# Float64 weights as a clipped 16-bit top and a 32-bit rest, and new lists of steps, in a sparse-attention and gated-MLP kernel

## The chip, the cores and the metric

The kernel runs on one core of a Trainium2 chip. The metric is the device time of one execution in microseconds (us). Engines are named PE (matrix), DVE (vector), ACT (scalar), POOL (GpSimd) and SP, which here only issues transfers.

## What is computed

```python
# attention: batch 8, 8 heads, 576 tokens, 64 wide
mask_local   = (rel >= 0) & (rel < 32)                      # heads 0 to 3
mask_strided = (rel >= 0) & (pos_k % 32 == pos_q % 32)      # heads 4 to 7
attn = softmax(where(mask, q @ k.T / 8, -1e9));  x = attn @ v      # x: 8 x 576 x 512
# gated MLP on x
h = gelu_tanh(x @ w_in)                    # 512 -> 1024
u, v = h[..., :512], h[..., 512:]
v_n = layernorm(v) * g_ln
v_s = einsum('ts,bsd->btd', w_sg, v_n) + b_sg
out = x + (u * v_s) @ w_out                # 512 -> 512
```

`w_in` and `w_out` arrive as float64. No engine reads float64 here: the kernel sees each weight as two 32-bit words and makes a float32 from them, then a rounded high part and a low part (`wih`/`wil`, `woh`/`wol`) for three-product matmuls.

## The kernel before

The eight batches run one behind the other, and the attention of the next batch is woven into the MLP of this one. Every step has a short name. Three lists of names, written out by hand in the file, fix the order: `START` (attention of batch 0, conversion of the weights, MLP of batch 0, attention of batch 1), `CYCLE` (MLP of batch b, attention of b+1; batches 1 to 6) and `LAST` (MLP of batch 7). Each engine works off its own instructions in the order of the list; transfers follow the list's order across the queues of SP and ACT. A `^` at a name picks the other choice of engine, queue or PSUM pool (`loads()`, `slow()`, `psum()`); `=`, `-`, `+` only say which batch is meant.

Names that matter below:

- `cl`, then `ca` to `ch`, convert one of 16 pieces of weight: 0 to 7 are 128x512 values of `w_in` (0 to 3 feed the `v` matmuls, 4 to 7 the `u` matmuls), 8 to 15 are 128x256 values of `w_out`. The piece's raw words lie in tile `stage` (0 to 7) or `cs` (8 to 15), the result in `cv`, `cx` or `cxl`. `cl` loads, `cg` writes the high part on ACT, `ch` the low part on POOL (or DVE with `^`).
- `TP`/`TC` turn rows of q and k on PE and copy them out (`qT`, `kT`); `SS`, `SL` are strided and local scores (`ss`, `sa`, `sr`); `MK`, `MX`, `SB`, `EX`, `SU`, `ML` are the softmax on `sms` and `sml`; `PL`, `PS` transpose the weights of attention (`ptl`, `pts`); `VA`/`VX`/`VY`, `PV`/`PW` multiply by v (`ol`, `os`); `XH`, `XL` write high and low parts of x (`xt`).
- In the MLP: `v1`, `v2`, `v` the v matmuls, `g` their gelu (`hv`), `ls`, `lr`, `lm`, `lh`, `ll` the layer norm (`lr` is a chain of 14 tiny POOL instructions that gives `y`; `lh` on ACT and `ll` on DVE write tile `vg`, and tile `t` for the last 64 tokens), `u` the u matmuls, `ug` their gelu on ACT, `s` the token-mixing matmuls (`sg`), which read `vg` and last of all `t`, `o` the output matmuls. A matmul's PSUM tile has two buffers in each of two pools, so the third use of a pool waits until the first was read.
- `LV`, `LQ`, `LP` load v, q and k.

The old conversion in numbers per piece: DVE takes the exponent field (`ca`), ACT rebiases it (`cb`), DVE puts the sign in and masks the mantissa (`cc`, two instructions), ACT scales it to 1.m (`cd`), the low word is added (`ce`, one DVE instruction, or ACT and POOL with `^`), and a product joins mantissa and exponent (`cf`, POOL or DVE).

Of the kernel before, what the change touches and what calls it, by code (L numbers as in the profile page):

```python
# [30 lines left out]
TC-:5 we=^ cd=:6 SS-^:2 cl=^:7 wt=:1 EX-:5 ML-:4 TC^:2 SU-^:5 MK-:2 cg=:0 TZ:0 ch=:0 ce=^:6
ML-^:5 TP:3 ca=:4 TZ:1 MX-:2 ML-:3 wh=:1 TC:3 LV-:0 ca=:7 PL-:4 wm=:1 CL-^:4 cb=:4 PL-^:5 CL-:5
SB-^:2 LP:0 CM-:5 ch=:3 VX-:0 VY-:0 EX-:2 XR-:0 LV-:1 SU-:2 ML-^:2 cb=:7 TP^:0 XHa-:0 XLa-:0
TC:0 cb=:9 ce=^:8 cf=:8 TP:1 TC:1 PS-^:2 XHb-:0 cc=:9 XLb-:0 cf=^:6 cc=:4 CS-:2 cl=:5 SL^:0
ca=:5 SL:1 XD-:0 MK:0 VA-:1 XH-:1 XL-:1 cd=:4 cc=:7 LV-:2 PV-^:2 PW-:2 LP:2 cd=:9 XH-:2 ce=:9
wo= cb=:5 XR-:1 MX:0 PS-:3 SB:0 wp= CS-:3 XL-:2 XD-:1 va:0 XR-:2 vb:0 cd=:7 cl=^:13 TP^:4 TC:4
vc:0 LV-:3 PV-:3 cc=:5 EX:0 PW-:3 XH-^:3 ce=:4 cf=^:4 va:1 XL-:3 xt cg=:4 vd:0 g:0 XD-^:2 XR-:3
vb:1 ce=:7 LP:3 wl=^:0 cf=^:9 ls:0 TP:6 ch=:4 vc:1 cd=:5 ce=:5 LZ:1 cf=:7 cg=^:9 vd:1 ch=^:9
TP:7 lr^:0 v^:2 ca=^:13 TC:6 cg=:6 cf=^:5 g:1 TC:7 ls:1 cg=:7 cg=:5 cl=^:15 TP^:5 ch=:6 ch=^:5
SS^:3 ch=:7 TC:5 cb=:13 cc=^:13 u:2 vh XD-:3 vl TZ+:0 g:2 cd=:13 MK:3 lg= LV:1 ce=:13 lm:0  # L40
wt=^:0 cf=^:13 wl=^:4 rt cl=:10 lh:0 ls:2 lm:1 wh=:0 wm=:0 lr:1 lm:2 lh:1 SS:2 ug:2 u^:1 wl=:2
lr:2 ug:1 ll:0 ca=:10 wt=^:4 cb=:10 ca=:15 cb=:15 u:0 SU:0 wh=:4 cc=:10 cg=:8 wl=:3 cd=:10 wt=:2
LQ+:0 wm=:4 ug:0 ce=:10 cf=:10 MK:2 wh=:2 cc=^:15 wm=:2 cl=^:11 wt=^:3 wh=:3 lh:2 cg=:13 wm=:3
ML:0 ll:2 u:3 ll:1 cd=:15 ca=:11 PL:0 cb=:11 cc=:11 ch=:13 CL:0 ug:3 MX:3 s:3 sm:3 ce=^:15
cd=:11 ce=:11 s^:2 cf=:11 cg=:11 CM:0 cf=^:15 MX:2 SB^:3 SB^:2 s^:0 cg=:10 ch=^:11 sm:2 cl=^:12
ca=:12 s:1 EX:3 TZ+:1 sh:2 sl:2 SU:3 sh:3 cb=:12 LZ:0 LQ+:3 ch=:8 cc=:12 ch=^:10 sm:0 cl=:14
cg=:15 cd=:12 ca=:14 ce=^:12 cf=:12 sh:0 cg=:12 TQ+:0 LV:0 ML^:3 VA^:1 sm:1 sh:1 sl:1 XR:1 r
cb=:14 sl:3 cc=:14 EX:2 sl^:0 ch=^:15 LQ+:1 VA:0 PS:3 CS:3 o:0 ch=:12 cd=:14 o^:1 ce=:14 cf=^:14
# [53 lines left out]
def tile_sparse_attention_moe(  # L102
# [166 lines left out]
    def cv(i):  # L269
        pairs = conv[i].rearrange("p (n w) -> p n w", w=2)  # L270
        n = pairs.shape[1]
# [12 lines left out]
        return pairs[:, :, 0], pairs[:, :, 1], conv[i, "ex"]  # L284

    def cv_load(i):
        if i < 8:
            conv[i] = stage[:, i % 5]
        else:
            conv[i] = p1.tile([P, F2], I32, tag="ob", name=f"cs_{i}", bufs=2)  # L290
        loads().dma_start(conv[i], halves[i][0])

    def cv_field(i):

        w0, w1, ex = cv(i)
        dve.tensor_scalar(
            ex, w1, 20, 0x7FF, op0=ALU.logical_shift_right, op1=ALU.bitwise_and
        )

    def cv_exp(i):  # L300

        w0, w1, ex = cv(i)
        act.activation(ex, ex, AF.Relu, bias=ebias, scale=float(1 << 23))

    def cv_sign(i):

        w0, w1, ex = cv(i)
# [5 lines left out]
    def cv_one(i):  # L313

        w0, w1, ex = cv(i)
        act.activation(w1.bitcast(F32), w1, AF.Copy, bias=1.0, scale=float(2.0 ** -20))

    def cv_word(i):

        w0, w1, ex = cv(i)  # L320
        mf, low = w1.bitcast(F32), w0.bitcast(U32)
        if alt[0]:
            act.activation(w0.bitcast(F32), low, AF.Copy, scale=float(2.0 ** -52))
# [722 lines left out]
```

## Time and profile before

| | us |
|---|---|
| three runs | 574.88, 579.43, 582.8 (median 579.43) |
| the profiled execution | 579.7 |
| its span on the core | 577.5 |
| PE busy | 542.7 (94%) |
| DVE busy | 415.3 (72%) |
| ACT busy | 216.0 (37%) |
| POOL busy | 180.6 (31%) |

The span is what the trace covers; the 2.2 us around it are taken as fixed. All rows below have line L83, since one helper issues every instruction: they are told apart by the names of tiles.

### The profile page before, as it was taken

What the parts mean: (1) busy time and instruction counts of PE and PEld (TensorE: products, weight loads), DVE (VectorE), ACT (ScalarE), POOL (GpSimd) and SP (SyncE); (2) the same over time, 40 slices, a digit from 0 to 9 for tenths busy, and PEclk for the clock granted to TensorE, in tenths of its full rate; (3) what the DMA queues carried; (4) which work ended last, traced back from release to release, by engine and by line L of the source; (5) the groups of instructions that cost most, each with busy time, mean ns of one, the idle gap of its engine ahead of it and who ended that gap; (6) DMA issues with size and microseconds to landing.
All of it is one profiled execution on the core that took longest, in us unless ns stands there. A gap on an engine that the chain in (4) does not pass through costs nothing. (4 is left out here: it accounts for less than half of the span.)

```text
span 577.5 us, 17028 instructions
## 1 busy us (share of the span) xinstructions
PE 542.7 (94%) x7217; PEld 483.9 (84%) x7217; DVE 415.3 (72%) x702; ACT 216.0 (37%) x352; POOL 180.6 (31%) x431
## 2 busy tenths in 40 slices
...
GB/s 244 237 203 118 140 154 82 181 151 154 181 34 53 161 173 143 42 114 155 165 75 49 165 173 139 42 135 137 168 79 51 159 188 37 0 139 143 1 0 92
DMA packets 253678, 70.09 MB, mean 121 GB/s; under 512 B 237793, under 2 KB 239329, under 8 KB 253602
## 3 DMA queue, kind: packets, MB, share of 16 engines
...
q10 hardware_dynamic: 82032, 21.31, 16.5%
...
## 5 line engine op out<-in xcount | busy, mean ns | idle before, releaser
L83 PE MATMUL sg<-wsh,vg 128*128 128x288 f32 x512 | 112.8, 296 | 0.7 <-DVE wst L83 0.5
L83 PE MATMUL u<-xt,wih 128*128 128x288 f32 x512 | 105.5, 301 | 7.1 <-ACT u L83 6.9
L83 PE MATMUL o<-woh,vg 128*128 128x512 f32 x288 | 95.2, 400 | 0.0
L83 PEld LDWEIGHTS u<-xt,wih 128*128 128x128 f32 x512 | 83.1, 190 | 9.8 <-ACT u L83 8.4
L83 PEld LDWEIGHTS sg<-wsh,vg 128*128 128x128 f32 x512 | 85.7, 188 | 1.4 <-issue 0.7
L83 PE MATMUL v<-wih,xt 128*128 128x512 f32 x256 | 84.5, 400 | 0.1
L83 PE MATMUL u<-xt,wil 128*128 128x288 f32 x256 | 76.3, 298 | 1.0 <-DVE wil L83 1.0
L83 PE MATMUL sg<-wsl,vg 128*128 128x288 f32 x256 | 75.4, 295 | 0.0
L83 PEld LDWEIGHTS o<-woh,vg 128*128 128x128 f32 x288 | 53.6, 188 | 13.4 <-DVE vg L83 2.6
L83 PEld LDWEIGHTS v<-wih,xt 128*128 128x128 f32 x256 | 48.6, 190 | 10.8
L83 PE MATMUL o<-wol,vg 128*128 128x512 f32 x144 | 56.3, 391 | 0.0
L83 PE MATMUL v<-wil,xt 128*128 128x512 f32 x128 | 50.3, 393 | 0.0
L83 PEld LDWEIGHTS u<-xt,wil 128*128 128x128 f32 x256 | 48.7, 190 | 1.2 <-DVE wil L83 1.2
L83 DVE TENSOR_TENSOR ob<-o,xn 128x512 f32<-128x512 f32 x32 | 22.0, 688 | 37.7 <-PE o L83 34.1
L83 PEld LDWEIGHTS sg<-wsl,vg 128*128 128x128 f32 x256 | 48.3, 189 | 0.0
L83 ACT CAST vg<-gt 128x576 fp32r<-128x576 f32 (+2 forms) x48 | 22.2, 511 | 57.7 <-DVE gt L83 57.7
L83 DVE TENSOR_TENSOR gt<-sg,u 128x576 f32<-128x576 f32 x32 | 23.8, 743 | 23.3 <-PE sg L83 20.7
L83 DVE BATCH_NORM_STATS2 bnst<-hv 128x6 f32<-128x512 f32 (+1 forms) x40 | 27.0, 675 | 18.1 <-ACT hv L83 18.1
...
L83 POOL MEMSET v<- 32x128 f32 x16 | 3.1, 198 | 97.9 <-PE os L83 70.6
L83 ACT ACTIVATE vg<-hv,y 128x512 fp32r<-128x512 f32 x32 | 20.7, 712 | 33.6 <-POOL y L83 31.6
L83 DVE TENSOR_TENSOR vg<-gt,vg 128x576 fp32r<-128x576 f32 (+2 forms) x45 | 23.2, 554 | 12.1 <-ACT vg L83 12.1
...
## 6 DMA issues: line engine op xcount, KB each, us to landing
...
```

The lines of the kernel that those rows point to most:

```text
L83: ins = self.tc.keep_in_program_order(op(*args, **kwargs))
```

## The change

The transfer of a raw piece now lands two bytes further on, so that of each float64 the top 16 bits lie in one int16 and the middle 32 bits in one aligned word. The tiles `stage` and `cs` are two words longer per partition for that. The top is clipped (`ck`: POOL, or DVE with `^`), a second instruction subtracts the clipped from the bounded top and so rebiases exponent and sign at once (`cc`, DVE), ACT scales the difference by 2^19 into an int32 (`ca`), ACT scales the middle word by 2^-13 into an int32 (`cd`), and POOL adds the two int32 (`ce`). `cg` and `ch` stay.

```diff
-    stage = p1.tile([P, 5, 2 * F2], I32, tag="vg", name="stage")
+    stage = p1.tile([P, 5, 2 * F2 + 2], I32, tag="vg", name="stage")
...
-        loads().dma_start(conv[i], halves[i][0])
+        n = halves[i][0].shape[1]
+        loads().dma_start(conv[i].bitcast(I16)[:, 1 : 2 * n + 1], halves[i][0].bitcast(I16))
+
+    def cv_clip(i):
+        mid, top, ex = cv(i)
+        slow().tensor_scalar(
+            ex.bitcast(F32), top, -14336.0, 14336.0, op0=ALU.max, op1=ALU.min
+        )
+
+    def cv_signed(i):
+        mid, top, ex = cv(i)
+        dve.scalar_tensor_tensor(
+            ex.bitcast(F32), top, -18432.0, ex.bitcast(F32), op0=ALU.max, op1=ALU.subtract
+        )
...
-        dve.tensor_scalar(
-            ex, w1, 20, 0x7FF, op0=ALU.logical_shift_right, op1=ALU.bitwise_and
-        )
...
-        act.activation(ex, ex, AF.Relu, bias=ebias, scale=float(1 << 23))
...
-        dve.scalar_tensor_tensor(
-            ex, w1, -(1 << 31), ex, op0=ALU.bitwise_and, op1=ALU.bitwise_or
-        )
-        dve.tensor_scalar(w1, w1, 0xFFFFF, None, op0=ALU.bitwise_and)
...
-        act.activation(w1.bitcast(F32), w1, AF.Copy, bias=1.0, scale=float(2.0 ** -20))
...
-        if alt[0]:
-            act.activation(w0.bitcast(F32), low, AF.Copy, scale=float(2.0 ** -52))
-            pool.tensor_tensor(mf, mf, w0.bitcast(F32), op=ALU.add)
-        else:
-            dve.scalar_tensor_tensor(mf, low, float(2.0 ** -52), mf, op0=ALU.mult, op1=ALU.add)
...
-        slow().tensor_tensor(val, w1.bitcast(F32), val, op=ALU.mult)
...
+        act.activation(ex, ex.bitcast(F32), AF.Copy, scale=float(1 << 19))
...
+        act.activation(mid, mid.bitcast(U32), AF.Copy, scale=float(2.0 ** -13))
...
+        pool.tensor_tensor(ex, ex, mid, op=ALU.add)
```

All three lists are written anew. Of `CYCLE`, the first two lines:

```diff
-v1:0 r SL:0 SL:1 TQ:3 v1:1 MK:0 xt MX:0 v2:1 SB^:0 g:1 ls^:1 v2:0 g:0 v^:2 vh lr:1 ls:0 u:2 ug:2
-u^:3 vl^ lm:0 g:2 TQ:2 lr:0 LQ+:0 lh:0 lm^:1 SS^:2 lh:1 SS^:3 ug:3 u^:0 ug:0 ls^:2 MK^:3 ll:1
+v1:0 r SL:0 TQ:3 SL:1 MK:0 xt v1:1 MX:0 v2:1 SB^:0 g:1 ls^:1 lr:1 v2:0 v^:2 g:0 vh ls:0 u:2 vl^
+ug:2 lr:0 lm:0 g:2 TQ:2 LQ+:0 SS^:3 u^:3 lm^:1 ug:3 SS^:2 lh:0 lh:1 u^:0 ug:0 ls^:2 MK^:3 lr:2
```

What that does to the engines is shown at three places. A row is the instruction, its output tile, its inputs and its shape; the last number of a tile's name only counts tiles.

First place, ACT at the end of `START`, where batch 1's MLP begins. Before, the five transfers of `v_0` (the last two are shown) stand ahead of the table load and the gelu `hv_1`:

```order
L83 DMA v_0_1903<-in_v_dram 64x8x64
L83 DMA v_0_1903<-in_v_dram 32x2x64
L83 ACT_TABLE_LOAD
L83 ACTIVATE hv_1_2067<-v_1_2032 128x1024
L83 ACTIVATE hv_0_2088<-v_0_1939 128x1024
```

Now, at the same place on ACT:

```order
L83 DMA out_dram<-ob_1_1866 128x512
L83 DMA out_dram<-ob_0_1878 128x512
L83 ACT_TABLE_LOAD
L83 ACTIVATE hv_1_2030<-v_1_2002 128x1024
L83 ACTIVATE hv_0_2077<-v_0_1902 128x1024
```

The five `v_0` transfers have moved to SP's queue, between those of `v_2` and `rawq_2`; it is the only batch for which they stood on ACT.

Second place, ACT in `CYCLE` (batch 1; batches 2 to 6 read alike), from the gelu of `u_2` to that of `u_1`, before:

```order
L83 ACTIVATE u_2_2150<-u_2_2125 128x576
L83 ACTIVATE hv_2_2099<-hv_2_2099 64x512
L83 ACTIVATE vg<-hv_0_2088,y_0_2186 128x4x128 x2
L83 ACTIVATE vg<-hv_1_2067,y_1_2102 128x4x128 x2
L83 ACTIVATE u_3_2284<-u_3_2152 128x576
L83 ACTIVATE u_0_2311<-u_0_2286 128x576
L83 ACTIVATE t_97<-hv_2_2099,y_2_2322 64x512
L83 ACTIVATE t_94<-hv_2_2099,y_2_2322 64x512
L83 ACTIVATE u_1_2376<-u_1_2340 128x576
```

And now:

```order
L83 ACTIVATE u_2_2114<-u_2_2088 128x576
L83 ACTIVATE hv_2_2079<-hv_2_2079 64x512
L83 ACTIVATE u_3_2210<-u_3_2183 128x576
L83 ACTIVATE vg<-hv_0_2077,y_0_2117 128x4x128 x2
L83 ACTIVATE vg<-hv_1_2030,y_1_2040 128x4x128 x2
L83 ACTIVATE u_0_2274<-u_0_2249 128x576
L83 ACTIVATE u_1_2330<-u_1_2303 128x576
L83 ACTIVATE t_97<-hv_2_2079,y_2_2283 64x512
L83 ACTIVATE t_94<-hv_2_2079,y_2_2283 64x512
```

The gelu of `u_3` has moved ahead of the four `vg` writes, and that of `u_1` ahead of the two `t` writes. On DVE the low part of `t` now stands ahead of the mask of `ss_2` instead of behind it, and on PE `ss_3` ahead of `u_3`.

Third place, DVE in `START`, from behind the product that `ptl` waits for (`sml` by `sr_5`) to the product that `pts` waits for (`sms_98` by `sr_2`), before:

```order
L83 TENSOR_SCALAR cv_522<-stage 128x512
L83 TENSOR_REDUCE mx_2_526<-sms_98 100x16
L83 TENSOR_SCALAR cv_538<-stage 128x512
L83 TENSOR_TENSOR wsl<-wsgT_492,wsh 128x4x128
L83 TENSOR_TENSOR wst<-wsgT_492,wsh 64x128
L83 TENSOR_TENSOR sms_98<-sms_98,mx_2_526 100x16x36
L83 COPY ptl_5_557<-ptl_8_555 128x128
L83 STREAM_TRANSPOSE xs_0_606<-ol_0_568 128x576
L83 TENSOR_REDUCE sr_2_613<-sms_98 100x16
L83 TENSOR_SCALAR sr_2_613<-sr_2_613 100x16
L83 RECIPROCAL sr_2_613<-sr_2_613 100x16
L83 TENSOR_TENSOR sms_98<-sms_98,sr_2_613 100x16x36
```

And now:

```order
L83 TENSOR_TENSOR sml_330<-sml_330,sr_5_494 128x640
L83 TENSOR_SCALAR cv_513<-stage 128x512
L83 TENSOR_TENSOR sms_98<-sms_98,mx_2_500 100x16x36
L83 SCALAR_TENSOR_TENSOR cv_513<-stage,cv_513 128x512
L83 TENSOR_SCALAR cv_527<-stage 128x512
L83 SCALAR_TENSOR_TENSOR cv_527<-stage,cv_527 128x512
L83 TENSOR_TENSOR wsl<-wsgT_446,wsh 128x4x128
L83 TENSOR_TENSOR wst<-wsgT_446,wsh 64x128
L83 TENSOR_REDUCE sr_2_590<-sms_98 100x16
L83 TENSOR_SCALAR sr_2_590<-sr_2_590 100x16
L83 RECIPROCAL sr_2_590<-sr_2_590 100x16
L83 TENSOR_TENSOR sms_98<-sms_98,sr_2_590 100x16x36
```

The maximum `mx_2` has moved ahead of the first product; the copy and the transpose have moved behind the second, and two conversions' second steps have come in between.

In all, DVE has 36 conversion rows where it had 74, ACT 48 where it had 53, POOL 28 where it had 22.

## Rows read from the trace of the kernel before

**Rows 1.** The page, part 1: busy us, share of the span, instructions.
```profile
PE 542.7 (94%) x7217; PEld 483.9 (84%) x7217; DVE 415.3 (72%) x702; ACT 216.0 (37%) x352; POOL 180.6 (31%) x431
```
**Rows 2.** Windows: stretch, length, busy us per engine, PE clock, DMA share, GB/s.
```profile
10.00:50.00 40.00, 28.93 (x593) 24.19 (x594) 37.76 (x68) 24.19 (x45) 18.19 (x22) 1.00 0.96 214
157.60:161.00 3.40, 3.40 (x17) 3.40 (x17) 3.32 (x5) 1.33 (x2) 1.28 (x4) 0.55 0.50 78
```
**Rows 3.** What PE waited for, 0 to 100 us: total us, times, longest.
```profile
PE ptl L83 <- DVE sml L83: 1.9, 1, 1.9
...
PE pts L83 <- DVE sms L83: 1.3, 1, 1.3
...
PE u L83 <- DVE wil L83: 1.0, 1, 1.0
PE turnk L83 <- DVE sml L83: 0.9, 1, 0.9
PE ptl L83 <- POOL sml L83: 0.8, 1, 0.8
...
PE sg L83 <- DVE wst L83: 0.5, 1, 0.5
```
**Rows 4.** What PE waited for, 100 us to the end.
```profile
PE u L83 <- ACT u L83: 6.9, 5, 3.4
```
**Rows 5.** Timeline of batch 1's MLP: start, us, engine, instruction, idle before.
```profile
133.79 4.35 ACTq L83 DMA_DIRECT2D v<-in_v_dram  x5
...
139.47 1.94 ACT L83 ACTIVATE hv<-v 128x1024 f32<-128x1024 f32 x2
...
153.24 2.56 ACT L83 ACTIVATE vg<-hv,y 128x512 fp32r<-128x512 f32 x4 [7.10 <-POOL y L83]
...
160.26 0.74 DVE L83 SCALAR_TENSOR_TENSOR t<-hv,y,t 64x512 fp32r<-64x512 f32 x1
...
136.81 0.62 PE L83 MATMUL v<-wih,xt 128*128 128x512 f32 x2
...
156.38 0.54 PE L83 MATMUL u<-xt,wih 128*128 128x288 f32 x2 [3.40 <-ACT u L83]
...
162.78 0.29 PE L83 MATMUL sg<-wsh,t 128*128 128x288 f32 x1
```
**Rows 6.** Timeline of batch 3's MLP, the same places, as a later batch runs.
```profile
291.38 0.63 ACT L83 ACTIVATE u<-u 128x576 f32<-128x576 f32 x1
...
291.38 0.74 DVE L83 SCALAR_TENSOR_TENSOR t<-hv,y,t 64x512 fp32r<-64x512 f32 x1
...
287.49 0.53 PE L83 MATMUL u<-xt,wih 128*128 128x288 f32 x2 [0.69 <-ACT u L83]
...
292.36 0.29 PE L83 MATMUL sg<-wsh,t 128*128 128x288 f32 x1
```
**Rows 7.** Groups of DVE instructions by form, 0 to 165 us: count, busy us, mean ns.
```profile
L83 DVE TENSOR_TENSOR cv<-stage,cv 128x512 f32<-128x512 f32 x6 | 6.0, 1008 | 0.1
L83 DVE TENSOR_SCALAR cv<-stage 128x512 int32<-128x512 int32 x8 | 5.6, 702 | 1.4 <-DMA stage<-in_moe_w_in_dram 1.4
L83 DVE SCALAR_TENSOR_TENSOR stage<-stage 128x512 f32<-128x512 uint32 x6 | 4.0, 675 | 0.0
...
L83 DVE TENSOR_SCALAR stage<-stage 128x512 int32<-128x512 int32 x8 | 3.7, 460 | 0.3
...
L83 DVE TENSOR_SCALAR cs<-cs 128x256 int32<-128x256 int32 x8 | 2.8, 348 | 0.3
...
L83 DVE SCALAR_TENSOR_TENSOR cs<-cs 128x256 f32<-128x256 uint32 x5 | 2.1, 424 | 0.3 <-ACT cs L83 0.2
```
**Rows 8.** Groups of POOL instructions by form, 0 to 165 us.
```profile
L83 POOL TENSOR_TENSOR cv<-stage,cv 128x512 f32<-128x512 f32 x2 | 2.6, 1308 | 0.1
...
L83 POOL TENSOR_TENSOR stage<-stage 128x512 f32<-128x512 f32 x2 | 2.1, 1038 | 0.2 <-ACT stage L83 0.2
...
L83 POOL TENSOR_TENSOR cs<-cs 128x256 f32<-128x256 f32 x3 | 1.8, 614 | 17.8 <-ACT cs L83 17.8
```

More of the change, by code (lines that the diff above doesn't have):

```diff
@@ L10 @@
 F32R = mybir.dt.float32r
+I16 = mybir.dt.int16
 I32 = mybir.dt.int32
@@ L31 @@
[L31 to L48, printed above, removed]
@@ new lines @@
+LP-^:2 SB-^:3 TC-:2 TZ-:1 TP-^:3 ck=:9 MK-:4 ca=:2 cc=:9 MX-:4 TC-:3 SL-:1 wb= SB-:4 cl=:6
+ck=^:6 cc=:6 EX-:4 ca=:6 EX-:3 ce=:2 cl=^:4 MK-:5 wc= cg=:2 wd= LZ-:1 ce=:3 wl=:1 TP-:4 MX-:5
+LP:1 ce=:0 SU-^:4 SU-:3 TP-:5 SB-:5 cg=:3 ch=^:2 LZ-:0 cd=^:8 TC-:4 TP^:2 we=^ cl=^:7 wt=:1 TZ:1
+TC-:5 EX-:5 ML-:4 SS-^:2 cg=:0 TZ:0 SU-^:5 MK-^:2 MX-^:2 ML-^:5 ch=:0 TP:3 TC^:2 ck=^:4 SB-^:2
+cc=^:4 wh=:1 cd=:6 TC:3 LV-:0 ck=^:7 PL-:4 cc=:7 CL-^:4 wm=^:1 ca=:4 PL-^:5 CL-:5 LP:0 ch=:3
+VX-:0 EX-:2 SU-:2 ML-^:2 VY-:0 TP^:0 LV-:1 XHa-:0 ca=:9 XLa-:0 XR-:0 ce=:8 TC:0 TP:1 TC:1 XHb-:0
@@ new lines @@
+PS-^:2 XLb-:0 CM-:5 ce=:6 CS-:2 cl=:5 ck=^:5 SL^:0 cc=:5 ca=:7 XD-:0 SL:1 MK:0 VA-:1 XH-:1 XL-:1
+cd=:4 LV-:2 PV-^:2 PW-:2 LP:2 cd=:9 XH-:2 wo= ca=:5 XR-:1 MX:0 ML-:3 SB:0 PS-:3 wp= CS-:3 XL-:2
+XD-:1 va:0 LV-:3 vb:0 TP^:4 XR-:2 cd=:7 cl=^:13 TC:4 vc:0 EX:0 PV-:3 PW-^:3 XH-^:3 ce=:4 XL-:3
+xt va:1 cg=:4 vd:0 XD-^:2 ch=:4 g^:0 XR-:3 LP:3 wl=^:0 vb:1 ce=:9 TP:6 vc:1 cg=^:9 ls:0 vd:1
+cd=:5 ce=:7 TP:7 ch=^:9 LZ:1 lr^:0 ck=^:13 v^:2 cc=:13 TC:6 cg=:6 g:1 TC:7 ls:1 ce=:5 cg=:7
+cg=:5 ch=^:5 cl=^:15 TP^:5 ch=:6 lg= SS^:3 lm:0 cd=:13 ca=:13 TC:5 vh ch=:7 u:2 XD-:3 TZ+:0 vl
@@ new lines @@
+MK:3 g:2 ce=:13 wt=^:0 wl=^:4 cl=:10 SS:2 lh:0 ls:2 lm^:1 wh=:0 lr:1 ug:2 lh^:1 u^:1 wl=:2 lr:2
+ug:1 ll:0 ck=^:10 LV:1 ck=^:15 wt=^:4 cc=^:10 wl=:3 ca=:10 wm=:0 cc=:15 lm:2 wh=:4 ca=:15 u:0
+cg=:8 SU:0 cd=:10 wt=:2 wm=:4 LQ+:0 ug:0 ce=:10 MK:2 wh=:2 wm=:2 cl=^:11 wt=^:3 wh=:3 lh:2 u:3
+cg=:13 wm=:3 ML:0 ll:2 ll:1 cd=:15 PL:0 ck=^:11 cc=:11 ca=:11 CL:0 MX:3 s:3 ug:3 sm:3 cd=:11
+ce=:11 CM:0 cg=^:11 ce=:15 MX:2 SB^:3 ch=:13 cg=:10 s^:2 ch=^:11 SB^:2 s^:0 ch=:8 sm:2 cl=^:12
+ck=^:12 cc=:12 EX:3 TZ+:1 sh:2 sl:2 s:1 LZ:0 SU:3 cl=:14 sh:3 ca=:12 LQ+:3 sl:3 ch=^:10 sm:0
```

82 lines of the change are left out of this document (32 added, 50 removed).

## The prediction, made before the changed kernel ran

> **What bounds the kernel now.** The page's first part comes first: PE is busy for 542.7 of 577.5 us, DVE for 415.3, ACT and POOL far less [rows 1]. So PE bounds the whole, and only an edit that removes a hole on PE shortens it. The reader is to see, though, that 94% is an average. The windows come next: from 10 to 50 us PE is busy for only 28.93 of 40 us at the full clock, while DVE is busy for 37.76 and the DMA share is 0.96 [rows 2]. That opening stage is where weights are loaded and converted. Third come PE's waits, because they name who is last there: before 100 us DVE or POOL ends waits of 1.9 + 1.3 + 0.9 + 0.8 = 4.9 us for products and masks of the softmax (`sml`, `sms`), 1.0 us for `wil` and 0.5 us for `wst`, 6.4 us in all [rows 3]. After 100 us one kind stands out: `u` waiting for ACT's gelu of an earlier `u`, because its PSUM tile is still unread: 6.9 us in five waits, the longest 3.4 us [rows 4]. Two timelines show what that longest one is made of [rows 5, 6].
>
> **The change part by part, removed work on DVE.** The old conversion's mask, its low-word addition and its product go: 6.0 + 4.0 + 3.7 + 2.8 + 2.1 = 18.6 us in 33 instructions [rows 7]. Five more of the 38 rows that go are products of 128x256 and clips that go to POOL, less a low part that comes back; between five times the smallest row shown, 0.35 us, and five times the largest, 1.01 us, that is 1.7 to 5.0 us; I take 3.5, so DVE loses about 22 us. The two that stay per piece, clip and subtraction, take the places of the exponent field (0.70 us [rows 7]) and of the sign. Their 16-bit input is not in the trace. The clip is bounded by the mask's 0.46 us and the product's 1.01 us; I take the 0.70 of the instruction with the same strided input, so it comes out even. At the bounds 14 clips change the sum by -3.4 to +4.3 us, which lies under other work except in the opening.
>
> **Added work on POOL.** Sixteen additions come: nearest are POOL's own additions of the old conversion, 1.04 us for 128x512 and 0.61 us for 128x256, above them the product of 1.31 us [rows 8]. All at the low rows: 8 x 1.04 + 8 x 0.61 = 13.2 us; all at the high one 21.0 us. I take 1.31 for the large and 0.75 for the small, 16.5 us, and 1.5 us for two clips (0.6 to 1.3 each). Twelve instructions go: seven in the rows shown, 2.6 + 2.1 + 1.8 = 6.5 us, and five (four small products, a low part) between 0.61 and 1.31 us each, say 4.5 us. POOL gains about 7 us, nearly all in the first 110 us. ACT loses five instructions and is costed at nothing: it waits for others throughout.
>
> **The opening (`START`).** About half of the pieces are converted ahead of the product that `pts_2` waits for, so about 10 of the 22 us leave DVE before it, and the order shows `mx_2` ahead of two conversions where it stood behind one. That is more than the 4.9 us that PE waits for DVE and POOL there. The bounds are nothing and the whole 4.9 us. I take half, 2.5 us, for two reasons: POOL multiplies in the same chains and gets longer, and q and k rows still come from a DMA that is nearly full (share 0.96 [rows 2]), so a PE that is earlier meets the next transfer earlier. The 1.0 us for `wil` and the 0.5 us for `wst` I take whole, since their DVE work has fewer rows ahead of it (bounds nothing and 1.5). Together -4.0 us, between 0 and -6.4.
>
> **Batch 1's MLP.** ACT issues the five transfers of `v_0` from 133.79 us for 4.35 us; behind them stands the gelu `hv_1`, which begins at 139.47 although the last `v` matmul row that it can need begins at 136.81 [rows 5]. It is 2.66 us late (2.04 by that row's modelled end). Layer norm follows: ACT waits 7.10 us for `y` and writes `vg` from 153.24; the gelu of `u_3` is queued behind those writes, and PE's `u_1` waits 3.40 us until 156.38 [rows 5]. The change takes both causes away: the transfers go to SP, which only issues, and `u_3`'s gelu stands ahead of `vg`. So 3.40 us goes. More may go. [...] From `u_1` to the first matmul on `t` it took 162.78 - 156.38 = 6.40 us; batch 3 took 292.36 - 287.49 = 4.87 us for the same [rows 5, 6]. [...] Ceiling 4.93 us. What is late next is `t`: its low part ends at 160.26 + 0.74 = 161.00, PE reads it at 162.78, a slack of 1.78 us, while PE arrives up to 4.93 us earlier; `y` is earlier by 2.0 to 2.7 us, and 1.78 + 2.5 = 4.3. I take -4.3 us. If `y` came no earlier (the POOL chain of `lr` waits for something else than the gelu), 1.8 us would be left.
>
> **Batches 2 to 6 and the end.** The other four waits of `u` are 6.9 - 3.4 = 3.5 us [rows 4]. Here the stall moves and does not go: in batch 3 the low part of `t` begins at 291.38 and ends at 292.12, PE's matmul on it begins at 292.36, so the slack is 0.24 us only [rows 6]. With `u_1`'s gelu of 0.63 us now ahead of `t` on ACT, a PE that arrives 0.69 us earlier waits for `t` instead. I take -0.5 us for the four together, between +1.6 (0.63 - 0.24 = 0.4 us lost in each of four) and -3.5. `LAST` is costed at nothing: its few orders lie inside a PE without holes in the waits shown.
>
> **The sum.** -4.0 - 4.3 - 0.5 = -8.8 us. The profiled execution took 579.7 us (0.05% above the median of 579.43), so 579.7 - 8.8 = **570.9 us**.
>
> **Rivals.** *All gaps of the opening go (R1).* If DVE alone was last in the waits, the whole 6.4 us goes instead of 4.0. PE is idle for 40 - 28.93 = 11.1 us between 10 and 50 us [rows 2], of which the softmax waits hold 4.9; with 10 us less on DVE the rest may shrink as well, and if it does by the same amount again, 5 us more go: 570.9 - 2.4 - 5 = about 563. For it: DVE's conversion rows show hardly any idle time ahead of them (0.0 to 0.3 us in all but one group [rows 7]), so DVE has always work. Against it: the DMA share of 0.96 [rows 2], which DVE's relief doesn't change.
>
> *POOL takes DVE's place (R2).* The additions of several pieces now stand ahead of low parts (`wil`) on POOL, at 1.31 us each, where PE waited 1.0 us for `wil` already [rows 3, 8]. If three or more are queued there, 4 us, the opening's gain is given back and the `wil` wait grows by about 1: 570.9 + 4.0 + 1.1 = 576. Against it: POOL is busy for only 180.6 of 577.5 us [rows 1].
>
> *The shifted transfers slow down (R3), on the other side.* Each raw row now lands two bytes off a word. Eight pieces of 512 KB and two of 256 KB are loaded in the opening, 4.72 MB, at 214 GB/s [rows 2] 22 us of all queues, while PE waits for what follows. If such a landing takes twice the time, those 22 us are added: 570.9 + 22 = 592.9 us. It eats the whole gain from a factor of 1.4 (8.8 of 22) and makes the kernel slower by over 2% (591.0 us) from 1.9. For it: DMA is the fullest resource there, and its word landing was aligned before. Against it: rows stay contiguous, 4096 and 2048 bytes each. No row shows a misaligned transfer.
>
> [...]
>
> **How the numbers follow.** My forecast (own range 566 to 575, from 4.9 us more gain to 4 less): 0.45. R1 (558 to 566): 0.20. R2 (575 to 580): 0.22. R3 (580 and above): 0.13. The range 561 to 580 leaves out R3 and the lower part of R1, about 0.17. Some 2% is what a measurement of this kernel can tell from no change; that is 567.8 and 591.0 us. Faster: R1 and the low end of the forecast, 0.27. Slower: the half of R3 from the factor of 1.9, 0.07, and no more than 0.01 of the rest, 0.08. Same: 0.65.
>
> **What would show it.** Conversion rows on DVE down to about 35 in 0 to 165 us and their sum by about 22 us; if the clip's row is 1.0 us, the gain of the opening is smaller. In PE's waits before 100 us, `ptl` and `pts` at half or less; a new `u <- POOL wil` of 2 us or more speaks for R2. The first landings of `stage`: if their time from issue or the DMA share at 10 to 50 us grows by half, R3 is on. In batch 1 `hv_1` on ACT begins within 0.5 us of its matmuls, `vg` 2 to 2.7 us earlier against them, `u <- ACT u` is gone, and no half clock follows. In batches 2 to 6 `u <- ACT u` is replaced by `sg <- DVE t`, of nearly the same size. The forecast is wrong if the opening's waits pass to DMA or POOL with no loss of length, or if the four later stalls go without a successor.

## The result, and the profile after

The changed kernel takes 574.55 us where the kernel before takes 579.31 us, medians over the same number of runs: a ratio of 0.9915, 95% interval 0.9887 to 0.9942. That is 0.85% faster, 4.9 us of 579.3. One of the changed kernel's 18 runs (607.45 us, mean granted clock 0.847) ran in a slow state and is left out of the ratio. The forecast was 570.9 us (8.8 us faster), its range 561 to 580. The sign and the range hold; a little over half of the gain came. The profiled execution took 573.37 us, with a span of 571.6 us beside 577.5.

Page, part 1, of the changed kernel (answers to [rows 1]):

```profile
PE 539.9 (94%) x7217; PEld 482.9 (84%) x7217; DVE 397.2 (69%) x664; ACT 213.7 (37%) x347; POOL 192.7 (34%) x437
```

DVE fell by 415.3 - 397.2 = 18.1 us and POOL rose by 192.7 - 180.6 = 12.1 us. The forecast had 22 and 7. The load on POOL is larger than taken. The relief of DVE is not smaller: from 0 to 165 us its conversion rows fall from 74 to 36 and from 44.8 to 19.6 us, by 25 us. But rows that the change did not touch got longer, these four most of all, before and after:

```profile
L83 DVE TENSOR_TENSOR sms<-sms,mx 100x576 f32<-100x576 f32 x4 | 3.1, 784 | 0.0
...
L83 DVE TENSOR_TENSOR sms<-sms,mx 100x576 f32<-100x576 f32 x4 | 5.3, 1319 | 0.0
```

Where the time went is read off PE by milestones: the start of the first `v` matmul of batch 1 (the opening ends), the first matmul on `t` of batch 1, that of batch 6, and the last matmul of all. Each is the start of a row in PE's timeline; the lengths between them, in us:

| kernel | opening | batch 1 to `t` | `t` of batch 1 to `t` of batch 6 | rest |
|---|---|---|---|---|
| before | 126.7 | 36.1 | 324.1 | 86.6 |
| changed | 124.1 | 31.9 | 325.7 | 85.9 |
| difference | -2.6 | -4.2 | +1.6 | -0.7 |
| forecast | -4.0 | -4.3 | -0.5 | 0 |

The timeline of ACT and PE in batch 1 of the changed kernel, the places of [rows 5] (start, us, engine, instruction, idle before):

```profile
134.57 1.03 ACT L83 ACTIVATE hv<-v 128x1024 f32<-128x1024 f32 x1 [1.29 <-PE v L83]
...
148.59 2.56 ACT L83 ACTIVATE vg<-hv,y 128x512 fp32r<-128x512 f32 x4 [1.54 <-POOL y L83]
...
155.94 0.40 PE L83 MATMUL sg<-wsh,t 128*128 128x288 f32 x1 [0.72 <-DVE t L83]
```

The gelu `hv_1` waits for PE alone now, nothing of ACT's stands ahead of it. `vg` is written 24.5 us after the stage's first matmul (148.59 - 124.1), where it was 26.5 (153.24 - 126.7). The wait for `u` is gone, 0.72 us for `t` is left, and the granted clock stays at 1.00 from 140 to 155 us.

PE's waits of the changed kernel, 0 to 100 us (answers to [rows 3]; total us, times, longest):

```profile
PE ptl L83 <- DVE sml L83: 3.6, 1, 3.6
...
PE u L83 <- DVE wil L83: 1.6, 1, 1.6
...
PE sa L83 <- DVE mx L83: 0.8, 1, 0.8
```

And from 160 to 490 us, batches 2 to 6 (answers to [rows 4]):

```profile
PE sg L83 <- DVE t L83: 2.8, 5, 0.6
```

In the opening the 4.9 us of softmax waits have not halved. The waits on `sml` and `sms` have come together in one of 3.6 us, 0.8 us has moved to `mx`, and the `wil` wait has grown from 1.0 to 1.6 us. In the later batches `u <- ACT u` has become `sg <- DVE t` five times, as foreseen. That exchange is not what made the stretch longer. PE's windows over it, before and after (columns as in [rows 2]):

```profile
162.78:486.91 324.13, 320.16 (x4444) 287.26 (x4442) 235.46 (x375) 109.23 (x168) 96.22 (x254) 1.00 0.56 117
...
155.94:481.69 325.75, 322.50 (x4442) 287.66 (x4442) 237.12 (x376) 110.72 (x168) 97.66 (x254) 1.00 0.55 117
```

PE's idle time falls from 324.13 - 320.16 = 4.0 us to 325.75 - 322.50 = 3.3 us; its busy time rises by 2.3 us, for the same work in another order.

### The profile page after: what moved, and what is told of

The parts are those of the page before. It is cut to its first block, busy times and chain, and to the rows that moved or that the text cites. A ratio compares the mean times of both kernels' runs of the same rounds, so it can differ in the third digit from the quotient of the medians.

```text
span 571.6 us, 17007 instructions
## 1 busy us (share of the span) xinstructions
PE 539.9 (94%) x7217; PEld 482.9 (84%) x7217; DVE 397.2 (69%) x664; ACT 213.7 (37%) x347; POOL 192.7 (34%) x437
## 4 chain that ended last, share of the span: by engine, by line
PE 77%; DVE 11%; issue 5%; POOL 4%; ACT 3%; ACTq 0%; POOLq 0%; DVEq 0%
PE v L83 17%; PE o L83 16%; PE u L83 16%; PE sg L83 15%; PE ol L83 3%; PE os L83 3%; PE sa L83 2%; PE pts L83 2%; POOL nt L83 2%; DVE sr L83 2%; DVE vg L83 2%; PE ss L83 1%; DVE cv L83 1%; DVE t L83 1%; DVE gt L83 1%
## 5 line engine op out<-in xcount | busy, mean ns | idle before, releaser
L83 DVE TENSOR_TENSOR ob<-o,xn 128x512 f32<-128x512 f32 x32 | 22.0, 689 | 44.8 <-PE o L83 41.5
L83 ACT ACTIVATE u<-u 128x576 f32<-128x576 f32 x32 | 20.6, 648 | 50.2 <-PE u L83 50.2
L83 DVE TENSOR_TENSOR vg<-gt,vg 128x576 fp32r<-128x576 f32 (+2 forms) x45 | 28.2, 654 | 15.4 <-ACT vg L83 15.3
```

Of the source, the lines that this page charges most:

```text
L83: ins = self.tc.keep_in_program_order(op(*args, **kwargs))
```

## The experiments

First the numbers of all runs. The ratio is against the kernel before, run on the same chip; the lengths are those of the table above, from the one profile of each.

| run | us | ratio, 95% interval | opening | batch 1 | 2 to 6 | rest |
|---|---|---|---|---|---|---|
| b_lv | 577.01 | 0.9945 (0.991 to 0.998) | 125.5 | 33.9 | 324.9 | 86.5 |
| b_ug3 | 579.44 | 1.000 (0.996 to 1.0039) | 127.7 | 33.8 | 323.0 | 86.5 |
| b_both | 576.61 | 0.9955 (0.992 to 0.999) | 124.5 | 32.5 | 323.2 | 87.0 |
| b_newcl | 579.22 | 0.9975 (0.9936 to 1.0015) | 128.2 | 33.1 | 325.6 | 85.7 |
| a_tfirst | 571.58 | 0.9863 (0.9797 to 0.9929) | 127.9 | 31.9 | 323.1 | 85.4 |
| a_ptl | 575.49 | 0.9924 (0.9891 to 0.9956) | 123.9 | 31.8 | 326.0 | 85.9 |
| a_align | 575.09 | 0.9922 (0.9884 to 0.9959) | 126.5 | 31.9 | 325.5 | 86.2 |
| a_oldlists | 584.53 | 1.0107 (1.0041 to 1.0172) | 134.4 | 36.3 | 324.8 | 86.8 |
| b_lists | 575.62 | 0.9923 (0.9892 to 0.9954) | 127.2 | 33.3 | 324.5 | 85.8 |
| a_tfirst5 | 572.30 | 0.9860 (0.9824 to 0.9896) | 126.2 | 31.9 | 323.4 | 85.8 |
| a_noadd | 571.32 | 0.9852 (0.9813 to 0.989) | 121.6 | 31.9 | 325.4 | 85.5 |
| b_less | 575.87 | 0.9938 (0.9908 to 0.9969) | 124.2 | 38.1 | 325.2 | 86.2 |

One thing must be seen before any row is compared. Up to its end, the opening of the kernel before, of b_lv, b_ug3, b_both, b_newcl and b_lists is one and the same program, but for five transfers late in b_lv, b_both and b_lists, and it took 124.5 to 128.2 us, 126.6 in the mean. The opening of the changed kernel, of a_tfirst and of a_tfirst5 is one program too, and took 124.1, 127.9 and 126.2 us, 126.1 in the mean. Batch 1 took 31.8 to 32.0 us in all six runs with the new `START` and `CYCLE`; b_lv and b_lists have 1.1 to 1.3 us of other waits in it, of which more below. The later batches repeat to about 1 us. So a difference of 2.6 us between two profiles of the opening proves nothing, and there the medians and the waits have to decide.

**b_lv: the transfers of v_0 alone.**

```diff
-XD:2 od:1 os:0 od:0 LV+^:0 LQ+:2 XL:2 LV+:1
+XD:2 od:1 os:0 od:0 LV+:0 LQ+:2 XL:2 LV+:1
```

> Kernel before with one edit: the five v_0 transfers of batch 1 go to SP's queue. My theory (they hold up the gelu hv_1 on ACT, and with it y): hv_1 begins within 0.5 us of its matmuls, the vg writes come 2.0 to 2.7 us earlier, PE's wait of 3.40 us for u falls to about 1, and the first matmul on t of batch 1 comes 2 to 4 us earlier; later batches keep that. Rival (y is set by POOL's own order, and the gelu was not last): vg moves by under 0.7 us and the time stays.

ACT's timeline of this run:

```profile
137.55 1.03 ACT L83 ACTIVATE hv<-v 128x1024 f32<-128x1024 f32 x1 [2.15 <-PE v L83]
...
151.38 2.56 ACT L83 ACTIVATE vg<-hv,y 128x512 fp32r<-128x512 f32 x4 [4.92 <-POOL y L83]
```

The wait of ACT for `y` falls from 7.10 to 4.92 us, PE's wait for `u` from 3.40 to 1.4, and the stage is 2.2 us shorter. PE's waits from 125 to 160 us show that more was gained:

```profile
PE u L83 <- ACT u L83: 1.4, 1, 1.4
PE sr L83 <- DVE xt L83: 0.7, 1, 0.7
PE sa L83 <- DVE xt L83: 0.6, 1, 0.6
```

The two waits for `xt`, 1.3 us, stand at the very start of the stage, at 129 and 131 us; the kernel before has none there. From the first `u` matmul of the batch to the first on `t` it took 162.78 - 141.59 = 21.2 us before and 159.39 - 141.91 = 17.5 us here, 3.7 us less. The theory holds, for the stage at the lower end of its 2 to 4 us and behind those waits at the upper.

**b_ug3: the gelu of u_3 alone.**

```diff
-u^:3 vl^ lm:0 g:2 TQ:2 lr:0 LQ+:0 lh:0 lm^:1 SS^:2 lh:1 SS^:3 ug:3 u^:0 ug:0 ls^:2 MK^:3 ll:1
+u^:3 vl^ lm:0 g:2 TQ:2 lr:0 LQ+:0 ug:3 lh:0 lm^:1 SS^:2 lh:1 SS^:3 u^:0 ug:0 ls^:2 MK^:3 ll:1
```

> Kernel before with one edit: in CYCLE the gelu of u_3 stands ahead of the four vg writes on ACT. My theory: the 3.40 us wait of batch 1 goes, but t is no earlier, so the first matmul on t gains only its slack of 1.8 us (up to 3.3 if the half clock of 157 to 161 us goes as well); batches 2 to 6 lose u <- ACT u and gain as much sg <- DVE t, so they stay within 0.5 us in sum. Rival (the gelu's place is the whole cause): batch 1 gains 3.4 to 4.9 us and the later batches another 2 to 3.

Batch 1 is 2.3 us shorter (expected 1.8 to 3.3), and in its place PE waits 1.8 us for `t`. Batches 2 to 6 are 1.1 us shorter, more than the 0.5 allowed, less than the rival's 2 to 3. The run time shows none of it (1.000, 0.996 to 1.0039); by the stages 3.4 us should be gone, and the interval's lower end is 2.3 us. What takes it back is not settled: the opening of its profile is 1 us longer than the mean of its siblings.

**b_both.** The two edits together.

> Kernel before with both edits, v_0 on SP and the gelu of u_3 ahead of vg. My theory: together 4.0 to 4.9 us at batch 1's first matmul on t, more than either alone, since each edit takes away one of two limits that lie one behind the other. Rival: one of the two edits alone gives all of it, the second adds less than 0.5 us.

PE's timeline of this run at the end of the stage:

```profile
157.00 0.40 PE L83 MATMUL sg<-wsh,t 128*128 128x288 f32 x1 [1.37 <-DVE t L83]
```

The stage is 3.6 us shorter, a little less than the 4.0 expected, and more than either alone (2.2 and 2.3). That last comparison misleads. Up to the gelu of `u_3`, b_lv and b_both are the same program, and the 1.3 us for `xt` of b_lv lie ahead of it; b_both happens to have no such wait. From the first `u` matmul of the batch to the first on `t`, which is free of it, the kernels took

| before | b_ug3 | b_lv | b_both | b_newcl | b_lists | changed |
|---|---|---|---|---|---|---|
| 21.2 | 18.9 | 17.5 | 17.3 | 18.0 | 17.0 | 17.0 |

So the transfers alone give 3.7 us, the gelu alone 2.3, and both 3.9: the second edit turns the 1.4 us for `u` into 1.37 us for `t` and adds 0.2 us. That is the rival's picture, and the run times agree with it (577.01 us for the transfers, 579.44 for the gelu, 576.61 for both). PE waits 1.37 us for `t` where the changed kernel waits 0.72: there `lr:1`, a chain on POOL, also stands earlier in `CYCLE`. No run moves `lr:1` alone, so that this is the reason is not shown.

**b_newcl.** The kernel before with the lists `CYCLE` and `LAST` of the changed one, in whole.

> Kernel before with the new lists CYCLE and LAST only (START and the conversion as before). Theory from the changed kernel's trace: the new CYCLE costs 0.3 to 0.4 us in each of batches 2 to 6 (sg <- DVE t in the place of u <- ACT u, as the gelu of u_1 stands ahead of t), some 1.6 us in all, LAST gains 0.7, batch 1 gains about 1.8. Rival: the loss in batches 2 to 6 comes from START's end state or the clock, and they stand as in the kernel before.

Batch 1 gains 3.0 us without the move of `v_0`, more than the 1.8 expected; batches 2 to 6 lose 1.5 us, the rest gains 0.9. The loss in the later batches belongs to the new `CYCLE`, whatever the opening was: with the old `CYCLE` that stretch took 324.1, 324.9, 324.8 and 325.2 us (before, b_lv, a_oldlists, b_less), with the new one 325.7, 325.6, 326.0, 325.5 and 325.4 (changed, b_newcl, a_ptl, a_align, a_noadd). In the mean it is 0.9 us. That `t` in the place of `u` is the reason, as the theory says, does not follow: b_ug3 has the old `CYCLE` with that exchange and nearly the idle time of the changed kernel (3.0 and 3.3 us), and took 323.0 us. What differs is PE's busy time, 320.0 us there and 322.5. Matmuls of `ss` hold 1.1 us of it (6.80 and 7.87 us) and those of `o` 0.5 (68.14 and 68.60), the same in number; why the new order makes them longer is open.

**a_tfirst and a_tfirst5: t ahead of the gelu of u_1.**

```diff
-ll:1 TZ+:0 u^:1 ll:0 ug:1 lm:2 lh:2 ll^:2 MK^:2 MX:2 EX:0 SU^:0 s^:1 SB:2 s^:0 MX:3 rt^ TQ+^:0
+ll:1 TZ+:0 u^:1 ll:0 lm:2 lh:2 ug:1 ll^:2 MK^:2 MX:2 EX:0 SU^:0 s^:1 SB:2 s^:0 MX:3 rt^ TQ+^:0
```

> Changed kernel with one edit: in CYCLE the gelu of u_1 stands behind the two t writes on ACT again. Theory: sg <- DVE t (3.5 us in six waits) falls under 1 us, batches 2 to 6 get 2.5 to 3.5 us faster, some 0.5% against the changed kernel. Rival (t is set by POOL's y or DVE, or the later gelu holds up PE's next PSUM tile or the product on u_1): the waits change their name and the batches stay within 0.5 us.

> The kernel of a_tfirst once more, the changed kernel with the gelu of u_1 behind t, for a narrower interval beside the others. Theory: 571 to 572 us, 0.5% under the changed kernel's 574.6. Rival (its four runs were lucky): 573.5 to 575.

ACT's timeline in batch 3, first of the changed kernel:

```profile
283.33 0.65 ACT L83 ACTIVATE u<-u 128x576 f32<-128x576 f32 x1 [2.53 <-PE u L83]
283.88 1.32 ACT L83 ACTIVATE t<-hv,y 64x512 fp32r<-64x512 f32 x2
```

Then of a_tfirst5:

```profile
284.88 1.34 ACT L83 ACTIVATE t<-hv,y 64x512 fp32r<-64x512 f32 x2 [2.65 <-POOL y L83]
286.12 0.63 ACT L83 ACTIVATE u<-u 128x576 f32<-128x576 f32 x1
```

And PE's waits of a_tfirst5, 160 to 490 us:

```profile
PE sg L83 <- DVE t L83: 0.4, 1, 0.4
```

In the changed kernel `t` is released by the gelu ahead of it, and that waits for PE itself; in a_tfirst5 it is released by `y`, and the gelu of `u_1` comes behind it and nobody waits for it. The five waits of 2.8 us shrink to one of 0.4, and the stretch to 323.1 and 323.4 us, 2.3 to 2.6 us less. Both runs give 1.4% under the kernel before (0.9863 and 0.9860). Against the changed kernel's 0.9915 that is 0.5%; the intervals overlap a little, the stage shows it twice. This version beats the kernel before, and by the stage the changed one too.

**a_ptl: two steps of START put back.**

```diff
-SU^:5 MK-^:2 MX-^:2 ML-^:5
+SU^:5 MK-^:2 ML-^:5 MX-^:2
...
-ch=^:2
+ch=:2
```

> Changed kernel with two steps of START put back: on DVE the maximum mx_2 (0.75 us) stands behind the product that ptl waits for, and the low part of piece 2 (1.52 us on DVE) is on POOL again. Theory (DVE has just these 2.3 us ahead of that product that it had not before): ptl <- DVE sml falls from 3.6 us to about 1.3, and the first v matmul of batch 0 comes 1 to 2.3 us earlier; without that hole the half clock from 35.5 to 48 us goes too. Rival (POOL, with its additions, is last): the product waits for POOL instead, ptl stays above 3 us.

PE's waits of this run, 0 to 100 us:

```profile
PE ptl L83 <- DVE sml L83: 1.4, 1, 1.4
...
PE turnq L83 <- DVE wst L83: 1.3, 1, 1.3
...
PE ptl L83 <- POOL sml L83: 1.0, 1, 1.0
```

The wait does fall from 3.6 to 1.4 us, as the two instructions' 2.3 us say. Yet the kernel is no faster (0.9924 beside 0.9915), and the first `v` matmul of batch 0 starts at 53.3 us beside 53.1: 1.0 us has come up for POOL's product and 1.3 us for `wst`. The half clock stays as well; the granted clock is 0.70 from 10 to 50 us, where the changed kernel has 0.83. The theory had the wait's cause right and its worth wrong.

**a_align: the pieces land at a whole word.**

```diff
-conv[i].bitcast(I16)[:, 1 : 2 * n + 1]
+conv[i].bitcast(I16)[:, 2 : 2 * n + 2]
...
-ex.bitcast(F32), top, -18432.0, ex.bitcast(F32)
+ex.bitcast(F32), top, 0.0, ex.bitcast(F32)
...
-scale=float(1 << 19)
+scale=float(1 << 15)
```

> Changed kernel, but the raw pieces land four bytes on, at a whole word, and two constants are other ones so that the misread values stay finite: it converts the wrong bits of the weights, all instructions are the same ones. Theory: the landing at an odd half word costs nothing that can be seen: same time within 0.3%, the pieces' transfers take the same time within 10%. Rival (the shifted landing is slow, and ate part of the opening's gain): first matmul of v 1 us or more earlier, DMA share from 10 to 50 us lower by a tenth or more.

Time 575.09 beside 574.55 us, ratio 0.9922 beside 0.9915. The windows from 10 to 50 us of this run, columns as in [rows 2]:

```profile
10.00:50.00 40.00, 25.54 (x593) 22.22 (x594) 33.93 (x59) 22.33 (x42) 25.75 (x33) 0.70 0.80 210
```

And of the changed kernel:

```profile
10.00:50.00 40.00, 28.02 (x622) 24.42 (x624) 33.74 (x61) 22.00 (x42) 26.44 (x33) 0.83 0.83 216
```

The aligned landing moves 210 GB/s at a DMA share of 0.80, the other one 216 at 0.83: the same bytes per share. This landing is still four bytes off the place of the kernel before, which moved 214 GB/s at a share of 0.96 [rows 2], so against no shift at all the rate isn't lower either. The odd landing costs nothing that can be seen here, and R3 is out.

**a_oldlists: the new conversion in the old order.** `START` of before, with each old step replaced by its successor, and the old `CYCLE` and `LAST`. The start of the list:

```diff
-mk= mp= cl=:3 ca=:3 LP-^:3 cb=:3 cc=^:3 cl=:1 ca=:1 cb=:1 TZ-:0 cc=:1 cd=:3 cd=:1
+mk= mp= cl=:3 ck=^:3 LP-^:3 cc=:3 ca=:3 cl=:1 ck=^:1 TZ-:0 cc=:1 ca=:1 cd=:3 cd=:1
```

> New conversion in the old lists: START of before with each old step replaced by its successor (field by clip on DVE, sign by subtraction and scaling, product by POOL's addition), CYCLE and LAST of before. It tells what the conversion alone is worth. Theory: the softmax waits of 4.9 us shrink by half or more, since DVE is relieved by the same 22 us and nothing is put in their place; 2 to 5 us at the first matmul of batch 1, then batch 1's stall as before. Rival (POOL takes DVE's place): low parts and softmax products on POOL come late, and it stands within 1 us of before or behind it.

The rival won: slower by 1.07% (0.41 to 1.72%). The opening of its profile is 7.8 us longer than the mean of the old one; that profile is of a run of 588.51 us where the median is 584.53, so the usual loss is smaller. POOL's timeline of this run:

```profile
34.55 1.17 POOL L83 TENSOR_TENSOR sms<-sms,sr 100x576 f32<-100x576 f32 x1
35.66 1.28 POOL L83 TENSOR_TENSOR wil<-cv,wih 128x512 fp32r<-128x512 f32 x1
36.88 0.75 POOL L83 TENSOR_TENSOR cx<-cx,cs 128x256 int32<-128x256 int32 x1
37.56 1.30 POOL L83 TENSOR_TENSOR cv<-cv,stage 128x512 int32<-128x512 int32 x1
```

DVE's and PE's timeline over the same time:

```profile
35.05 4.50 DVE L83 TENSOR_TENSOR sml<-sml,sr 128x640 f32<-128x640 f32 x1
...
39.70 1.30 PE L83 MATMUL ptl<-ident,sml 128*128 128x128 f32 x5 [5.11 <-DVE sml L83]
```

This is the most telling place of the study. The product on DVE takes 4.50 us; the same product took 0.81 us in the changed kernel (shown below). It begins within the first of four POOL instructions with two inputs that run back to back, two of them the new additions, and ends 0.69 us after the last of them does (37.56 + 1.30 = 38.86, 35.05 + 4.50 = 39.55). That it stood still until then and did its work in the rest is the author's estimate from these times; no row shows it. PE waited 5.11 us for it. The kernel before shows the same in small, on DVE and then POOL:

```profile
36.74 2.60 DVE L83 TENSOR_SCALAR cv<-stage 128x512 int32<-128x512 int32 x1
...
36.15 1.68 POOL L83 TENSOR_TENSOR sms<-sms,sr 100x576 f32<-100x576 f32 x1
37.80 1.26 POOL L83 TENSOR_TENSOR wil<-cv,wih 128x512 fp32r<-128x512 f32 x1
```

That DVE row has a single tensor input and its seven siblings take 0.43 us in the mean (eight in 5.6 us, [rows 7]), so two inputs on DVE's side were not needed for its 2.60 us. And it goes the other way too. In the changed kernel the product took its 0.81 us in the midst of an addition, and it was the addition that took 2.78 us where the one above took 1.30:

```profile
34.95 2.78 POOL L83 TENSOR_TENSOR cv<-cv,stage 128x512 int32<-128x512 int32 x1
...
35.43 0.81 DVE L83 TENSOR_TENSOR sml<-sml,sr 128x640 f32<-128x640 f32 x1
```

**a_noadd: the changed kernel without POOL's additions.**

```diff
-        pool.tensor_tensor(ex, ex, mid, op=ALU.add)
+        pass
```

> Changed kernel without POOL's 16 additions, so the weights lack their lower bits. Theory (POOL's instructions with two inputs hold up those of DVE and stretch them, and so take back what DVE saves): the subtraction's mean on DVE falls from 0.92 to under 0.75 us and that of wil from 1.09 towards 0.7, ptl <- DVE sml falls from 3.6 us to under 2, and the time falls by 1.5 to 4 us against the changed kernel. Rival (transfers of q and k and PE's clock bound the opening, DVE and POOL have room): DVE's rows may shrink, but the time stays within 1 us.

DVE's and POOL's groups by form, 0 to 165 us, of the changed kernel (count, busy us, mean ns, idle before):

```profile
L83 DVE SCALAR_TENSOR_TENSOR cv<-stage,cv 128x512 f32<-128x512 int16 x8 | 7.4, 919 | 2.0 <-POOL cv L83 1.8
...
L83 DVE TENSOR_SCALAR cv<-stage 128x512 f32<-128x512 int16 x7 | 3.0, 422 | 7.4 <-DMA stage<-in_moe_w_in_dram 7.4
L83 DVE TENSOR_TENSOR wil<-cv,wih 128x512 fp32r<-128x512 f32 x2 | 2.2, 1092 | 0.0
...
L83 POOL TENSOR_TENSOR cv<-cv,stage 128x512 int32<-128x512 int32 x8 | 12.5, 1566 | 0.2
...
L83 POOL TENSOR_SCALAR cv<-stage 128x512 f32<-128x512 int16 x1 | 2.1, 2059 | 8.1 <-DMA stage<-in_moe_w_in_dram 8.1
```

And of a_noadd:

```profile
L83 DVE SCALAR_TENSOR_TENSOR cv<-stage,cv 128x512 f32<-128x512 int16 x8 | 6.3, 781 | 2.0 <-POOL cv L83 1.8
...
L83 DVE TENSOR_TENSOR wil<-cv,wih 128x512 fp32r<-128x512 f32 x2 | 1.3, 642 | 0.0
```

Windows of a_noadd, 10 to 50 us, and then PE's first wait for DVE there:

```profile
10.00:50.00 40.00, 30.70 (x686) 26.89 (x690) 32.16 (x61) 22.56 (x43) 17.24 (x27) 1.00 0.82 214
```

```profile
PE ptl L83 <- DVE sml L83: 1.8, 1, 1.8
```

Without the additions the subtraction's mean falls from 919 to 781 ns (expected under 750), that of `wil` from 1092 to 642, the wait for `sml` from 3.6 to 1.8 us, and the `wil` wait goes. The kernel takes 571.32 us, 3.2 less than the changed one, and its opening of 121.6 us is the shortest of all. So the additions cost about 3 us, by the medians of four runs and of 18, whose intervals (0.9813 to 0.989 and 0.9887 to 0.9942) meet at the edge. The one profile of the opening can't carry this alone: its granted clock was 1.00 from 10 to 50 us, the changed kernel's 0.83. But a run of the changed kernel at a mean clock of 1.00 still took 573.29 us. Whether by holding DVE or by POOL's own time between the two scalings and the high part, this run does not part; that DVE's rows were longer with the additions than without (919 and 781 ns, 1092 and 642) speaks for the first.

**b_less: the kernel before without the DVE rows that went.**

```diff
-        dve.tensor_scalar(w1, w1, 0xFFFFF, None, op0=ALU.bitwise_and)
+        pass
...
-            dve.scalar_tensor_tensor(mf, low, float(2.0 ** -52), mf, op0=ALU.mult, op1=ALU.add)
+            pass
...
-        slow().tensor_tensor(val, w1.bitcast(F32), val, op=ALU.mult)
+        alt[0] or pool.tensor_tensor(val, w1.bitcast(F32), val, op=ALU.mult)
```

> Kernel before without the DVE rows that the change removed and with nothing in their place: no mask (16), no low-word addition on DVE (11), no product on DVE (10), so the weights are wrong; POOL and ACT as before. It is the relief of 22 us alone. Prediction's step: the opening gets 2.5 to 6.4 us faster, 573 to 577 us. Theory now (DVE's relief is worth it, POOL's growth took it back): the same, 3 to 5 us, and the softmax waits of 4.9 us at half or less. Rival (relief of DVE is worth nothing, since transfers and clock bound): within 1 us of before, waits for rowq and rowk longer instead.

Its windows, 10 to 50 us:

```profile
10.00:50.00 40.00, 29.17 (x622) 24.46 (x626) 32.12 (x56) 24.04 (x45) 18.20 (x22) 0.81 0.98 217
```

575.87 us, ratio 0.9938: the relief alone is worth 3.6 us (1.8 to 5.3). Of the 4.9 us of softmax waits 3.1 us are left (2.4 for `sml`, 0.7 for `sms`), not the half or less that was expected. The profile is of a run of 579.7 us, 3.8 above the median: its batch 1 took 38.1 us, with 0.9 us of waiting for `kT` and, behind a wait for `u` of 3.4 us as in the kernel before, `u` matmuls on `wil` of 0.44 us each from 155 to 160 us, which had taken 0.29 to 0.30 us just ahead of the wait. DVE's busy time from 10 to 50 us falls by 37.76 - 32.12 = 5.6 us, in the changed kernel by 37.76 - 33.74 = 4.0 only. So the step from DVE's relief to a gain was sound; it was POOL's growth that was booked too low.

**b_lists: old conversion and START, best lists.** The edit of b_lv, the new `LAST`, and the `CYCLE` of a_tfirst.

> Old conversion and old START, with v_0 on SP, the new LAST, and the new CYCLE in which the gelu of u_1 stands behind the two t writes again. Theory (the new conversion and the new START are worth nothing, all the gain is in the order of the batches): as fast as a_tfirst, about 571.5 us, within 1.5. Rival (START and conversion give the 2.6 us that the one profile shows at the first v matmul of batch 1): 574 us or more.

575.62 us, not 571.5. It stands 3.3 us above a_tfirst5, which differs in conversion and `START` alone. By the profiles batch 1 holds 1.4 of it (33.3 and 31.9; 1.1 us are waits for `xt` at its start), the batches 2 to 6 1.1 (324.5 and 323.4), and some 1 us is the opening's (127.2 and 126.2). The rival's 574 us or more is what came, but not by its reason: conversion and `START` are worth 3.3 us in all, and only about 1 us of that lies in the opening.

## Why the prediction came out as it did

**What bounds.** Right: PE, with 94% before and after, and the two holes that were named are those that moved.

**Batch 1, -4.3 us.** Right, 4.2 by the stages and for the stated reasons: both causes act, and `t` is what is late next (0.72 us). They overlap, though: from the first `u` matmul on, the transfers give 3.7 us alone, the gelu's place 2.3, both 3.9, so the transfers are nearly all of it. The half clock behind the hole is gone too: the granted clock of this stage was 0.95 in the kernel before, with 0.50 from 158 to 161 us, and is 1.00 in the changed one. The 4.93 us of the forecast are the hole's 3.40 and the 6.40 - 4.87 = 1.53 us by which batch 1 was longer than batch 3 from `u_1` to `t`. At a granted clock of 0.73 the kernel before took those 6.40 us; at 1.00 the changed one took 155.94 - 150.30 = 5.64 us, 0.72 of it waiting for `t`.

**Batches 2 to 6, -0.5 us.** Wrong in sign: +0.9 us in the mean of several runs, +1.6 in the pair of profiles. The exchange of waits was named, `t` queued behind the gelu of `u_1`, and it came out about as forecast: PE's idle time falls by 0.7 us. So that the +1.6 of the pair equals the worst bound is luck; the bound was worked out for the waits. What failed is a term that was put at nothing without a reason: PE's own busy time in the new order, which rose by 2.3 us. Putting `t` ahead of the gelu of `u_1` gains 2.3 to 2.6 us (a_tfirst, a_tfirst5), so the queue is worth undoing, but it is not what the new order lost.

**The opening, -4.0 us.** This is the step that failed most: -2.6 us in the two profiles, but about -1: -0.5 by the means of equal programs (126.6 and 126.1), -0.9 by b_lists, and -0.9 and -1.7 at an equal granted clock from 50 to 60 us (changed against b_lv and b_both at 1.00, a_tfirst5 against b_ug3 and b_newcl at 0.66). The DVE relief was sound by itself (b_less 3.6 us). What failed is the line "POOL gains about 7 us". It gained 12.1 us: the additions took 1566 ns each for the large pieces where 1.31 us was taken, and the two clips 2.06 and 1.53 us where 1.5 was taken for both. More than that, POOL was costed as an engine apart. Beside its instructions with two inputs a product on DVE took 4.50 us for 0.81 (a_oldlists), and beside DVE's rows one of its additions took 2.78 us for 1.30 (changed kernel), so an addition took back time here on the engine that was relieved. Removing the additions gives 3.2 us back (a_noadd).

`wil` was taken as a whole gain of 1.0 us and became a loss of 0.6. That the low part of one piece moved to DVE is not the reason: a_ptl takes it back to POOL and the wait stays at 1.6 us. Without the additions it is gone (a_noadd). DVE's rows in the changed kernel ahead of the `wil` that `u` waits for:

```profile
64.96 1.27 DVE L83 TENSOR_SCALAR va<-mv 128x2 f32<-128x2 f32 x1
66.27 1.22 DVE L83 TENSOR_SCALAR y<-va 128x2 int32<-128x2 int32 x1
...
68.90 1.20 DVE L83 SCALAR_TENSOR_TENSOR nt<-nt,va 128x2 f32<-128x2 f32 x1
...
72.49 0.66 DVE L83 TENSOR_TENSOR wil<-cv,wih 128x512 fp32r<-128x512 f32 x1
```

The first three take 0.15 to 0.17 us each in the kernel before; here they took 1.20 to 1.27 us, beside an addition and two low parts on POOL, and each ended 0.02 us after one of those (66.23 and 66.21, 67.49 and 67.47, 70.10 and 70.08 us). That is rival R2 in a milder form, on DVE instead of on POOL: it was given 0.22 and 576 us, and 574.55 lies between it and the forecast. With the old order (a_oldlists, 584.5 us) it would have come in full and beyond: by these two runs the new `START` is what makes the new conversion pay.

**LAST, nothing.** The stretch from `t` of batch 6 on gained 0.7 us; the small wait of 0.4 us for `t` in batch 7 went.

**R1 and R3.** R1 fell with the waits that stayed. R3 fell with a_align: nearly the same share, rate and time (0.80 and 0.83, 210 and 216 GB/s, 575.09 and 574.55 us).

So the sum of about -1.0 - 4.2 + 0.9 - 0.7 = -5.0 us meets the 4.9 us measured. The opening's part in it is known to about 0.5 us only, so the agreement to a tenth is luck.
